# The opening of an attention and mixer kernel: small tables on GpSimd's queue, the first head loaded in halves

## The chip, the cores and the metric

The kernel runs on one core of one Trainium2 chip. A core has five engines that run side by side and meet only through semaphores: TensorE (PE) multiplies matrices into PSUM, VectorE (DVE) and ScalarE (ACT) do elementwise work, GpSimd (POOL) does some of that too, and SyncE (SP) issues transfers. SyncE, ScalarE and GpSimd each have a queue on which transfers (DMAs) are issued; all of them run on the same 16 DMA engines. The metric is the device time of one execution in microseconds (us).

## The reference

Two layers follow each other. The first is block-sparse attention over 4 batches of 8 heads, with 768 tokens of 64 elements and blocks of 32 tokens:

```python
scores = scale * np.matmul(q, k.transpose(0, 1, 3, 2))
mask = np.abs(blk_i - blk_j) <= window
mask = mask | (blk_i == 0) | (blk_j == 0) | (blk_i == n_blocks - 1) | (blk_j == n_blocks - 1)
for qb in range(n_blocks):
    for kb in sampled_blocks[qb]:
        mask[qb * block:(qb + 1) * block, kb * block:(kb + 1) * block] = True
scores = np.where(mask, scores, -1000000000.0)
attn = softmax(scores)
out = np.matmul(attn, v)
```

The 24 x 3 array sampled_blocks says which three extra key blocks each of the 24 query blocks sees. Its values are known only at run time, so the mask is computed on the chip.

The second is a residual mixer on the result x (4 x 768 x 512):

```python
a1 = alpha1 * x + beta1
u = x + lam * einsum('ts,bsd->btd', w_tok, a1)
a2 = alpha2 * u + beta2
out = u + lam * (np.maximum(a2 @ w_ch1, 0.0) @ w_ch2)
```

## The kernel before

**Stages.** Two heads make a pair, and there are 16 pairs. For a pair, q and k are brought to 16-bit types (tile rel), transposed (tiles qx and kx, 64 rows for the head dimension), multiplied to scores in PSUM (L601, later L611), turned into exponentials by ScalarE (L622, tile eT) and multiplied with v (L638). The token product of the mixer (L740) and its two channel products (L805, L974, L884) follow, batch by batch, between the pairs. The order of all this work is one list, ORDER, written out by hand; each engine carries out its part of it in that order, and nothing reorders it at run time.

**The mask of the first pairs.** For the first five pairs the mask is part of the score product: qx and kx get 24 more rows (the slice MB, rows 64 to 87). In kx these rows say which block a key belongs to (the constant ind), in qx they hold 0 where the query may see the block and -400 where not. They are made in the prologue: block_mask (L320 and L326) compares sampi, the sampled blocks, with the block numbers in eqt, a table of block numbers and the fixed mask, and reduces to mbm, 24 x 24. Two products (mask_bias, L357) spread it over 768 tokens, one half each, and VectorE (L366) and ScalarE (L369) write the two halves to qx.

**The prologue around the change.** Only what runs ahead of the list is edited:

- SyncE issues q of the first head (L290), the identity for the transposes (identb, L292), sampi (L294), ind for kx of slot 0 (L296), then q and k of the second head (L297, L298). ScalarE issues k of the first head (L291), the table eqt (L293) and ind for slot 3 (L295), and then loads its function table.
- TensorE runs products with a zero tile, called fillers here (zero, L310): 7 of 512 columns and 2 of 128 ahead of the first transposes, 12 of 128 ahead of the first score.
- first_cast (L340 on ScalarE for k, L342 on VectorE for q) casts the first head in two halves of three slots of 64 elements each. Both halves of q come first on VectorE, then block_mask.
- TensorE transposes the first three slots (flatA), then the last three (flatB), and then makes the mask products. VectorE and ScalarE copy the parts to kx and qx (L363 to L371).
- GpSimd's first instruction of its own copies 24 elements of q to a tile called hold (L378), which is used for nothing else. It waits for the first q, so all loads that GpSimd issues behind it (v, k and q of the following pairs, the token weights wtk, later the channel weights) start only then. GpSimd has 8 completion semaphores in turn; a load waits for the one 8 places ahead of it.

Of the kernel before, what the change touches and what calls it, by code (L numbers as in the profile page):

```python
# [14 lines left out]
I32 = mybir.dt.int32  # L15
# [5 lines left out]
S = 768  # L21
D = 64
BLK = 32
NBLK = S // BLK
# [3 lines left out]
P = 128  # L28
NT = S // P
HS = S // 2  # L30
# [172 lines left out]
def kernel(  # L203
# [19 lines left out]
    nc = tc.nc  # L223
# [19 lines left out]
    tabs_dr = nc.inline_tensor(tabs_np, name="tabs_c")  # L243
# [10 lines left out]
    sampi = pp.tile([P, 2 * NR], I32, name="sampi", tag="sampi")  # L254
    identb = pp.tile([P, P], BF, name="identb", tag="identb")
    qx = [pp.tile([P, S], BF, name=f"qx{i}", tag=f"qx{i}") for i in range(NQB)]
# [10 lines left out]
    eqt = pp.tile([P, NR + 2, NBLK], FP, name="eqt", tag="eqt")  # L267
# [4 lines left out]
    MB = slice(D, KC)  # L272


    def pair_ap(src, b, n):
        return src[b, 2 * n : 2 * n + 2].rearrange("h (p o) d -> p h (o d)", o=NT)
# [4 lines left out]
    def bank(i, shape, dt=FP):  # L281
        t = psum[:, ts(i, 512)]
        if dt != FP:
            t = t.bitcast(dt)
        t = t[:, 0 : int(np.prod(shape[1:]))]
        return t if len(shape) == 2 else t.rearrange("p (o c) -> p o c", o=shape[1])

    q2f = wk.tile([P, 2, NT * D], FP, name="q2f", tag="hts", bufs=2)
    k2f = wk.tile([P, 2, NT * D], FP, name="k2f", tag="hts", bufs=2)
    nc.sync.dma_start(q2f[:, 0, :], pair_ap(q, 0, 0)[:, 0, :])  # L290
    nc.scalar.dma_start(k2f[:, 0, :], pair_ap(k, 0, 0)[:, 0, :])  # L291
    nc.sync.dma_start(identb[:], ident_dr.ap())  # L292
    nc.scalar.dma_start(eqt[MB, 0:2, :], tabs_dr.ap().rearrange("p (r c) -> p r c", r=2))  # L293
    nc.sync.dma_start(sampi[MB, :], sampled_blocks.bitcast(I32))  # L294
    nc.scalar.dma_start(kx[3][MB, :], ind_dr.ap())  # L295
    nc.sync.dma_start(kx[0][MB, :], ind_dr.ap())  # L296
    nc.sync.dma_start(q2f[:, 1, :], pair_ap(q, 0, 0)[:, 1, :])  # L297
    nc.sync.dma_start(k2f[:, 1, :], pair_ap(k, 0, 0)[:, 1, :])  # L298
# [10 lines left out]
    def zero(w, i):  # L309
        nc.tensor.matmul(bank(i, [P, w]), warm[:, 0:P], warm[:, 0:w], start=True, stop=True)  # L310

    for _ in range(7):
        zero(512, 6)
    for _ in range(2):
        zero(P, 6)
    for t in vext:
        nc.vector.memset(t[:, :, :, D:VW], 1.0)
# [1 line left out]
    def block_mask():  # L319
        nc.vector.tensor_tensor(  # L320
            out=eqt[MB, 2 : 2 + NR, :],
            in0=sampi[MB, 0 : 2 * NR : 2].unsqueeze(2).broadcast_to([NBLK, NR, NBLK]),
            in1=eqt[MB, 0, :].unsqueeze(1).broadcast_to([NBLK, NR, NBLK]),
            op=ALU.is_equal,
        )
        nc.vector.tensor_reduce(  # L326
            out=mbm[MB, :],
            in_=eqt[MB, 1 : 2 + NR, :].rearrange("p r c -> p c r"),
            axis=mybir.AxisListType.X,
            op=ALU.max,  # L330
        )

    rels = {0: wk.tile([P, 2, NT, 2 * D], BF, name="rel", tag="rel", bufs=4)}

    def first_cast(a, lo=0, hi=NT):
        for i, src in enumerate((q2f, k2f)):
            sl = src[:, a, :].rearrange("p (o d) -> p o d", o=NT)[:, lo:hi, :]
            dst = rels[0][:, a, lo:hi, i * D : (i + 1) * D]
            if a == 0 and i == 1:
                nc.scalar.copy(out=dst, in_=sl)  # L340
            else:
                nc.vector.tensor_copy(out=dst, in_=sl)  # L342

    def transposes(rel, a, i, slots=range(NT)):
        tps = bank(i, [P, NT, P], BF)
        for o in slots:
            nc.tensor.transpose(tps[:, o, :], rel[:, a, o, :], identb[:])  # L347
        return tps.rearrange("p o c -> p (o c)")

    first_cast(0, 0, 3)  # L350
    first_cast(0, 3, 6)
    block_mask()
    bqs = {}

    def mask_bias(w):
        bqs[w] = bank((2, 7)[w], [P, 512])[0:NBLK, 0:HS]
        nc.tensor.matmul(bqs[w], mbm[MB, :], kx[3][MB, ts(w, HS)], start=True, stop=True)  # L357

    flatA = transposes(rels[0], 0, 0, range(0, 3))
    flatB = transposes(rels[0], 0, 1, range(3, 6))  # L360
    mask_bias(0)
    mask_bias(1)
    nc.vector.tensor_copy(out=kx[0][0:D, 0:P], in_=flatA[D:P, 0:P])  # L363
    nc.scalar.copy(out=qx[0][0:D, HS:S], in_=flatB[0:D, HS:S])
    nc.vector.tensor_copy(out=qx[0][0:D, 0:HS], in_=flatA[0:D, 0:HS])
    nc.vector.tensor_scalar(  # L366
        out=qx[0][MB, 0:HS], in0=bqs[0], scalar1=1.0, scalar2=BIG, op0=ALU.subtract, op1=ALU.mult
    )
    nc.scalar.activation(qx[0][MB, HS:S], bqs[1], AF.Identity, bias=-BIG, scale=BIG)  # L369
    nc.vector.tensor_copy(out=kx[0][0:D, P:HS], in_=flatA[D:P, P:HS])  # L370
    nc.vector.tensor_copy(out=kx[0][0:D, HS:S], in_=flatB[D:P, HS:S])  # L371
    for _ in range(12):
        zero(P, 6)
    for j in range(2, NQB):
        nc.sync.dma_start(qx[j][MB, :], qx[0][MB, :])

    hold = pp.tile([P, NBLK], BF, name="hold", tag="hold")
    nc.gpsimd.tensor_copy(out=hold[:], in_=q2f[:, 0, 0:NBLK])  # L378

    flag = pp.tile([P, 3 * NPAIRS], BF, name="flag", tag="flag")  # L380
    held = pp.tile([P, 3 * NPAIRS], BF, name="held", tag="held")
# [636 lines left out]
    for word in ORDER.split():  # L1018
        kind = word[: next(j for j, c in enumerate(word) if c.isdigit())]
        n, _, arg = word[len(kind) :].partition(":")  # L1020
# [35 lines left out]
```

## Time and profile before

| | us |
|---|---|
| runs: median of 3 (lowest to highest) | 293.21 (292.14 to 293.95) |
| profiled execution: time | 292.62 |
| profiled execution: span of the records | 290.8 |
| PE busy | 285.0 (98%) |
| DVE busy | 263.8 (91%) |
| ACT busy | 233.5 (80%) |
| POOL busy | 52.3 (18%) |

All durations come from the one profiled execution; its span is 1.8 us shorter than its time, for what lies around it. Four views are used. The chain of work that ended last goes back from the last instruction, at each step to what released it. The timeline lists instructions in order: start, length, engine, line, what is written from what, shape and count; a bracket says how long the engine sat idle before and what ended it. The DMA view gives each issue's size and its time to landing. The windows view gives busy time and DMA share for a stretch. A matmul's length in the timeline includes its way through the array, so the pace of products is read from start to start.

### The profile page before, as it was taken

The numbers are of one execution on the slowest core, as the hardware profiler recorded it, in microseconds if no ns is written. First come the engines' busy times: TensorE is split into PE (matmuls) and PEld (weight loads), VectorE is DVE, ScalarE is ACT, GpSimd is POOL, SyncE is SP. The second block draws the span as 40 slices with busy tenths as digits, with TensorE's granted clock in tenths as the row PEclk, the third lists the DMA queues.
The fourth block names the chain that finished last, engine by engine and source line by source line (L and its number), as shares of the span: only waits on it lengthen the run. The fifth ranks groups of instructions, "written<-read, shape, count | busy, mean of one in ns | idle before, by whom it ended". The sixth has DMA issues, their size and how long they took to land.

```text
span 290.8 us, 8517 instructions
## 1 busy us (share of the span) xinstructions
PE 285.0 (98%) x3542; PEld 214.8 (74%) x3542; DVE 263.8 (91%) x591; ACT 233.5 (80%) x349; POOL 52.3 (18%) x94
## 2 busy tenths in 40 slices
PE   8899999999999999999999999999999999999995
PEld 4677888665677788766677877888766788866884
DVE  5599998779999999999999999999999998699983
ACT  3999999849999999999999999968989860279400
POOL 5645754200521142024005000000000000000000
PEclk9999999999999999999999999999999999999999
DMA  6999999999684499499367002404210040330014
GB/s 161 178 233 223 196 206 190 203 218 182 120 112 30 53 119 135 77 176 116 43 183 146 9 2 56 83 5 47 38 74 0 16 115 0 148 144 1 2 42 176
DMA packets 48035, 30.97 MB, mean 107 GB/s; under 512 B 28972, under 2 KB 44092, under 8 KB 47996
## 3 DMA queue, kind: packets, MB, share of 16 engines
q0 software_dynamic: 15936, 15.21, 34.6%
q1 hardware_dynamic: 31412, 14.31, 23.0%
q10 hardware_dynamic: 648, 0.89, 0.9%
q8 instruction: 28, 0.46, 0.7%
q14 instruction: 11, 0.09, 0.1%
HBM read 31.19 MB, written 6.88 MB: 131 GB/s over the span
## 4 chain that ended last, share of the span: by engine, by line
PE 89%; ACT 8%; DVE 1%; issue 1%
PE psum L884 26%; PE psum L974 13%; PE psum L805 12%; PE psum L638 11%; PE psum L740 11%; PE psum L611 9%; ACT eT L622 6%; PE psum L601 4%; ACT hts L819 2%; PE psum L310 2%; PE psum L347 1%; PE psum L783 1%; DVE a1p L710 0%; PE psum L357 0%; ACT rel L396 0%
## 5 line engine op out<-in xcount | busy, mean ns | idle before, releaser
L622 ACT ACTIVATE eT<-psum 128x1024 f16<-128x1024 f32 (+1 forms) x145 | 140.1, 1028 | 9.4 <-PE psum L611 5.4
L632 DVE TENSOR_TENSOR eT<-eT,maskT 128x960 f16<-128x960 f16 x99 | 61.2, 650 | 0.0
L884 PEld LDWEIGHTS <-hts 128*128 128x128 bf16 x480 | 45.1, 98 | 8.5 <-issue 2.1
L638 PEld LDWEIGHTS <-eT 128*128 128x128 f16 x1152 | 44.4, 97 | 8.2 <-issue 1.7
L638 PE MATMUL psum<-vext,eT 128*128 128x65 f16 x1152 | 48.5, 193 | 0.0
L805 PE MATMUL psum<-uT,w1b 128*128 128x384 bf16 (+1 forms) x256 | 45.9, 327 | 0.1
L1000 ACT ACTIVATE snap<-psum,b1t 128x384 f32<-128x384 f32 x44 | 23.6, 581 | 17.7 <-PE psum L974 13.5
L740 PE MATMUL psum<-a1p,wtokT 128*128 128x128 bf16 x576 | 36.8, 219 | 0.2 <-DVE x_sb L749 0.2
L740 PEld LDWEIGHTS <-wtokT 128*128 128x128 bf16 x576 | 33.2, 98 | 4.1 <-DVE x_sb L749 0.8
L884 PE MATMUL psum<-w2t,hts 128*128 128x256 bf16 x288 | 35.8, 273 | 0.0
L843 DVE TENSOR_TENSOR x_sb<-x_sb,psum 128x256 f32<-128x256 f32 (+1 forms) x61 | 30.7, 514 | 4.7 <-PE psum L884 4.5
L805 PEld LDWEIGHTS <-w1b 128*128 128x128 bf16 x256 | 23.0, 98 | 16.1 <-ACT b1t L396 0.9
L819 ACT ACTIVATE hts<-psum,b1t 128x384 bf16<-128x384 f32 x53 | 29.1, 600 | 1.0 <-PE psum L805 0.5
L611 PE MATMUL psum<-qx,kx 64*128 64x256 bf16 x396 | 29.8, 272 | 0.0
L843 DVE TENSOR_TENSOR hts<-snap,psum 128x384 bf16<-128x384 f32 x48 | 24.7, 547 | 2.7 <-PE psum L974 2.3
L601 PE MATMUL psum<-qx,kx 88*128 88x512 bf16 (+1 forms) x120 | 25.7, 326 | 1.0 <-ACT eT L622 1.0
L884 PE MATMUL psum<-w2b,ss 128*128 128x256 bf16 x192 | 24.6, 273 | 0.0
L884 PE MATMUL psum<-w2b,hts 128*128 128x256 bf16 x192 | 24.4, 273 | 0.0
L611 PEld LDWEIGHTS <-kx 64*128 64x128 bf16 x396 | 15.2, 94 | 8.4 <-issue 3.7
L884 PEld LDWEIGHTS <-ss 128*128 128x128 bf16 x192 | 18.0, 98 | 3.8 <-issue 0.6
L749 DVE TENSOR_TENSOR x_sb<-x_sb,psum 128x384 f32<-128x384 f32 x32 | 17.4, 546 | 0.8 <-PE psum L740 0.5
L974 PEld LDWEIGHTS <-w1b 128*128 128x128 bf16 x128 | 12.1, 98 | 6.6 <-DVE hts L843 0.3
(98 smaller groups left out, 364.1 us busy)
## 6 DMA issues: line engine op xcount, KB each, us to landing
out_dram<-x_sb SPq DMA_DIRECT2D x17, 256.0 KB, 2.4
v<-in_v_dram POOLq DMA_DIRECT2D x16, 192.0 KB, 6.2
k<-in_k_dram POOLq DMA_DIRECT2D x15, 192.0 KB, 5.3
q<-in_q_dram POOLq DMA_DIRECT2D x15, 192.0 KB, 6.8
w2b<-in_moe_w_ch_dram POOLq DMA_DIRECT2D x4, 512.0 KB, 11.7
w1b<-in_moe_w_ch_dram POOLq DMA_DIRECT2D x4, 512.0 KB, 11.5
wtk<-in_moe_w_tok_dram POOLq DMA_DIRECT2D x3, 384.0 KB, 7.9
out_dram<-x_sb SPq DMA_DIRECT2D x2, 512.0 KB, 2.7
```

The lines of the kernel that those rows point to most:

```text
L601: nc.tensor.matmul(t[:, f : f + w], kx[h][0:KC, ts(jt, P)], qx[h][0:KC, c : c + w], start=True, stop=True,)
L611: nc.tensor.matmul(t[:, (2 * a + j) * TH : (2 * a + j + 1) * TH], kx[h][r, ts(2 * g + j, P)], qx[h][r, ts(th, TH)], start=True, stop=True,)
L622: nc.scalar.activation(eTs[n][:, c], t[:, c], AF.Exp, bias=EXPB, scale=SCALE)
L632: nc.vector.tensor_tensor(out=e, in0=e, in1=mask, op=ALU.min)
L638: nc.tensor.matmul(ops[key][:, t * VW : t * VW + D + 1], eTs[n][:, c : c + P], vext[n // NU % NV][:, a, jt, 0 : D + 1], start=(first and z ...
L740: nc.tensor.matmul(t[:, j, :], wtokT[:, s, ts(3 * g + j, P)], a1p[p][:, s, :], start=(s == 0), stop=(s == NT - 1),)
L805: nc.tensor.matmul(hps[i][:, 0:w], w1b[:, dk, ts(f, P)], uT[b][:, dk, hf * HS : hf * HS + w], start=(dk == 0), stop=(dk == 3),)
L819: nc.scalar.activation(hts[kk][:, f, :], t[:, 0:HS], AF.Relu, bias=b1t[:, f : f + 1], scale=1.0)
L843: nc.vector.tensor_tensor(out=out, in0=in0, in1=in1, op=op)
L884: nc.tensor.matmul(cps[b, q][:, side * HD : (side + 1) * HD], lhs[:, nk, :], rhs[:, nk, :], start=(z in (0, 6) and nk == 0), stop=(nk == H ...
L974: nc.tensor.matmul(chains[key], lhs[:, dk, ts(f, P)], rhs[:, dk, :], start=(z in (0, 1, 5) and dk == 0), stop=(dk == 1), skip_group_check= ...
L1000: nc.scalar.activation(dst, t, act, bias=bias, scale=1.0)
```

## The change

The two small loads that block_mask needs, sampi and eqt, move from SyncE's and ScalarE's queues to the head of GpSimd's queue, ahead of the copy to hold. The loads of the first head's q and k are each split into two transfers, of three slots each; the second halves are issued as the third transfer of their queues. The copy to hold reads the last 24 elements of q in place of the first 24.

On VectorE block_mask moves between the two casts of q. On TensorE the two mask products move between the transposes of the first half and those of the second, with three fillers of 128 columns ahead of them. ScalarE's mask bias (L369) moves ahead of its copy of the second half of q (L364). The fillers ahead of the first transposes become 4 of 512 columns and 3 of 128, and those ahead of the first score become 5.

```diff
-    nc.sync.dma_start(q2f[:, 0, :], pair_ap(q, 0, 0)[:, 0, :])
-    nc.scalar.dma_start(k2f[:, 0, :], pair_ap(k, 0, 0)[:, 0, :])
+    nc.gpsimd.dma_start(sampi[MB, :], sampled_blocks.bitcast(I32))
+    nc.gpsimd.dma_start(eqt[MB, 0:2, :], tabs_dr.ap().rearrange("p (r c) -> p r c", r=2))
+
+    def first_load(lo, hi):
+        cut = slice(lo * D, hi * D)
+        nc.sync.dma_start(q2f[:, 0, cut], pair_ap(q, 0, 0)[:, 0, cut])
+        nc.scalar.dma_start(k2f[:, 0, cut], pair_ap(k, 0, 0)[:, 0, cut])
+
+    first_load(0, NT // 2)
     nc.sync.dma_start(identb[:], ident_dr.ap())
-    nc.scalar.dma_start(eqt[MB, 0:2, :], tabs_dr.ap().rearrange("p (r c) -> p r c", r=2))
-    nc.sync.dma_start(sampi[MB, :], sampled_blocks.bitcast(I32))
     nc.scalar.dma_start(kx[3][MB, :], ind_dr.ap())
+    first_load(NT // 2, NT)
     nc.sync.dma_start(kx[0][MB, :], ind_dr.ap())
...
-    for _ in range(7):
+    for _ in range(4):
         zero(512, 6)
-    for _ in range(2):
+    for _ in range(3):
         zero(P, 6)
...
     first_cast(0, 0, 3)
+    block_mask()
     first_cast(0, 3, 6)
-    block_mask()
...
     flatA = transposes(rels[0], 0, 0, range(0, 3))
-    flatB = transposes(rels[0], 0, 1, range(3, 6))
+    for _ in range(3):
+        zero(P, 6)
     mask_bias(0)
     mask_bias(1)
+    flatB = transposes(rels[0], 0, 1, range(3, 6))
     nc.vector.tensor_copy(out=kx[0][0:D, 0:P], in_=flatA[D:P, 0:P])
-    nc.scalar.copy(out=qx[0][0:D, HS:S], in_=flatB[0:D, HS:S])
     nc.vector.tensor_copy(out=qx[0][0:D, 0:HS], in_=flatA[0:D, 0:HS])
...
     nc.scalar.activation(qx[0][MB, HS:S], bqs[1], AF.Identity, bias=-BIG, scale=BIG)
+    nc.scalar.copy(out=qx[0][0:D, HS:S], in_=flatB[0:D, HS:S])
...
-    for _ in range(12):
+    for _ in range(5):
         zero(P, 6)
...
-    nc.gpsimd.tensor_copy(out=hold[:], in_=q2f[:, 0, 0:NBLK])
+    nc.gpsimd.tensor_copy(out=hold[:], in_=q2f[:, 0, NT * D - NBLK :])
```

## The prediction

> **What bounds the kernel now.** I read the chain that ended last in order of time first, since the change touches only what runs before the first exponential. Start and length are in us.
>
> ```profile
> 1.19 3.38 PE psum L310 x9
> 4.57 0.64 PE psum L347 x6
> 5.21 0.74 PE psum L357 x2
> 5.95 1.15 PE psum L310 x12
> 7.10 0.23 PE psum L601
> ...
> 11.43 5.61 ACT eT L622 x6
> ...
> 25.52 1.03 ACT eT L622
> 26.55 0.05 issue
> 26.59 0.61 PE psum L601 x3
> ```
>
> Three stages: up to 7.1 us TensorE never stops, but two thirds of that time is filler (L310, products with a zero tile); then ScalarE's exponentials (L622) carry the chain; from 26.6 us on TensorE does, nearly to the end. A gain in the opening is worth only what reaches 26.6 us. The timeline tells what arrives there:
>
> ```profile
> 3.65 0.61 DVE L342 CAST rel<-q2f 128x192 bf16<-128x192 f32 x2 [2.42 <-DMA q2f<-in_q_dram]
> 3.68 0.20 POOL L378 CAST hold<-q2f 128x24 bf16<-128x24 f32 x1 [3.24 <-DMA q2f<-in_q_dram]
> 3.82 0.60 ACT L340 CAST rel<-k2f 128x192 bf16<-128x192 f32 x2 [0.35 <-DMA k2f<-in_k_dram]
> 3.83 0.84 POOL L414 DMA_DIRECT2D v<-in_v_dram  x1
> 4.32 0.23 DVE L320 TENSOR_TENSOR eqt<-sampi,eqt 24x72 f32<-24x72 int32 x1
> ...
> 19.75 0.51 PE L473 MATMUL psum<-identb,wtk 128*128 128x128 bf16 x6 [0.18 <-DMA wtk<-in_moe_w_tok_dram]
> ...
> 26.59 0.61 PE L601 MATMUL psum<-qx,kx 88*128 88x512 bf16 x3 [0.18 <-ACT eT L622]
> ```
>
> The brackets carry the argument. TensorE runs without a gap from 10.34 to 19.57 us, waits 0.18 us for a token-weight load, runs without a gap to 26.41, waits 0.18 us for ScalarE, and is the bound from there. So **two clocks arrive at 26.6 together**: the exponentials, which start with the first score, and GpSimd's stream of loads. The stream starts when the copy into hold (L378) sees the first q, and the DMA view has it full from then on (share 1.17 and 213 GB/s between 7.35 and 26.6 us): its loads land 5 to 10 us after issue, so a later start is a later landing.
>
> **The change, part by part.** Behind the prologue the instructions of every engine stand in the same order, so only its shift counts. Landing times below are the trace's landing records.
>
> *Halved loads.* Before, q was issued at 0.74 and landed at 3.63, k at 0.73 and 3.79 (2.9 and 3.1 us), the first packet 1.0 us after issue. Half the bytes take at least 1.0 for the start, half of the 1.5 us that the packets took, and 0.4 for completion: 2.15; at most the old 2.9. I take 2.5: first halves land at 3.25. ScalarE still issues three transfers and its table load (1.28, from 2.18) ends at 3.46, so k's first cast, not the load, sets the pace: 3.46 + 0.35, first transposes at about 3.9 instead of 4.36. The second q half is issued third on SyncE, where the sampled blocks were (1.64): landing between 3.8 and 4.4 by the same bounds. I take 4.0, near the lower one, because less lies ahead of it.
>
> *Blocks and table on GpSimd.* Two issues at about 0.73. GpSimd's one-dimensional issues take 0.54 to 0.58, the first load of all 0.84; the table is issued between 1.3 and 1.6. Issue to landing: the table on ScalarE's queue took 2.68 (1.18 to 3.86), the first GpSimd load 4.41 with 192 KB (3.83 to 8.25, first packet after 1.76). So the table lands between 4.0 and 6.0. It moves 4.5 KB, so the small load is the nearer row: 4.1.
>
> *Mask between the casts.* Call the start of the block comparison S: 4.1, where before it was 4.32. Now q's second cast is queued behind it on VectorE, and TensorE has the mask products ahead of the second transposes. From rows: comparison to reduction 0.26, reduction 0.31, on to the first product 0.25 (4.89 to 5.14), then 0.29 and 0.46 to what follows the second product, three transposes of 0.107 with 0.31 for the last to end, 0.06 and 0.47 for ScalarE's copy (L364, 5.24), 0.05 to the first score: S + 2.67 = 6.77. Before, it was 6.94: **0.17 us earlier**, break-even at S = 4.27. The second cast (S + 0.5 to S + 0.85) and VectorE's last key copy (before, 6.46 to 6.81, needed by later scores only) hide beside this. The k cast of the second half waits for its own half, 4.0 to 4.4, ahead of ScalarE's mask bias at S + 1.7, and is hidden.
>
> *Fewer fillers.* Out go 3 of 512 columns (0.427 each) and 3 net of 128 (0.107 to 0.056): 1.5 us of TensorE time. This is no gain of its own; it only lets the 0.17 us through, since before the 12 fillers ended at 6.94 while ScalarE's bias was done at 6.46. Their worth is the clock (below).
>
> *hold.* It now reads the last columns of q, the second half: 4.0 instead of 3.63. GpSimd's two added issues are done by 2.0, ahead of it. The stream starts **0.37 us later** (bounds 0.12 and 0.76), and v, k, q and the token weights queue behind.
>
> **Sum.** Exponentials: 26.59 - 0.17 = 26.42. Loads: 26.41 + 0.37 = 26.78. The later one decides: +0.19, 292.62 us of the profiled execution become 292.8. That execution lies 0.59 under the median of the runs (293.21), so on their scale **293.4 us**. Own range: stream bounds give 26.53 to 27.17, -0.06 to +0.58; with the spread of the runs shown (292.14 to 293.95) 292.6 to 294.2. No change that 1% (2.9 us, about what a measurement of this kernel can tell from no change) would show.
>
> **Rivals.**
>
> *A, gain kept (0.2).* The halves land at their lower bound (3.8) and the table at 4.0: stream +0.12, score 0.27 earlier. For it: packets at the opening move at 287 GB/s between 2 and 3 us, and less lies ahead of the halves. Against: the token-weight wait at 19.75, which caps any gain at 0.18 with the stream unmoved. Time: between -0.18 and +0.12, about 293.1.
>
> *B, TensorE stays slow (0.15).* Products start 427 ns apart for 512 columns and 107 for 128 until 6.60, 56 from 6.77 on: the pace doubles 5.5 us after the first product, though the granted-clock row shows 1.00 throughout. The fillers keep TensorE gapless until then. In the changed kernel they end at 3.2, transposes come at 3.9, and gaps follow before the products and the scores. If the 5.5 us count again from 3.9, the scores run at half pace from 6.8 to 9.4: 1.3 us of work lost. TensorE's idle stretch from about 9.4 to 10.34 takes up most, the exponential at 11.43 comes about 0.5 late: +0.5, 293.9; a second such stretch would cost up to 2 us more. Against: gaps of 0.4 to 0.7 us may not count. [...]
>
> *C, the table lands late (0.15), the slower side.* One mechanism: GpSimd's first transfers take the 4.41 us of its first load. It decides from S = 4.27. At S = 5.98 the first score comes at 8.65, 1.7 us late; the exponentials run back to back, and about 0.3 us of their waits at 17.0 to 25.5 are used up: +1.4, 294.6. q's second cast waits behind the comparison with all of VectorE. For it: a first packet after 1.76 against 1.02 on the other queues. Against: that load's 192 KB. [...]
>
> **Chances.** Forecast 0.5, A 0.2, B 0.15, C 0.15. The range reaches from A's low end to C: 292.3 to 294.8. Faster by over 1% needs more than the 0.18 us cap: 0.02. Slower by over 1% needs B's second stretch together with C: 0.07. Within 1%: 0.91.
>
> **What would show it.** Right: first score (L601) near 6.8, comparison (L320) near 4.1 and ended by the GpSimd load, hold near 4.0, the token-weight wait before 19.75 longer and later, TensorE reaching 26.4 without waiting for ScalarE. B: score products 213 ns apart for 256 columns instead of 109. C: VectorE idle ahead of L320 past 4.3. Wrong altogether: a difference that arises after 27 us, where nothing was moved.

## The result, and the profile after

The changed kernel is **slower by 1.0%**: 295.94 us median of 7 runs (294.75 to 297.26) against 292.99 us for the kernel before in the same runs, a ratio of 1.0098 with a 95% interval of 1.0073 to 1.0123. The forecast was 293.4 with a range of 292.3 to 294.8, so the time lies 1.1 us above the range. Its profiled execution took 295.44 us, with a span of 293.5 against 290.8.

The chain that ended last, of the changed kernel, in order of time (start, length, what; lines are those of the changed file, where L609 is the score product and L630 the exponential):

```profile
1.27 0.68 POOL sampi L290
1.96 3.03 DMA eqt<-tabs_c
...
5.08 0.24 DVE eqt L326
5.34 0.30 DVE mbm L332
...
7.61 2.74 PE psum L609 x9
10.36 0.64 PE psum L353 x6
10.99 0.85 PE psum L609 x2
11.85 0.80 PE psum L316 x2
12.65 1.61 PE psum L609 x5
14.28 5.61 ACT eT L630 x6
...
28.33 1.03 ACT eT L630
29.36 0.05 issue
29.41 0.61 PE psum L609 x3
```

Before, fillers held the chain to 7.1 us. Now it begins with the table's transfer on GpSimd's queue, and the stretch that ScalarE carried from 7.35 us on belongs to TensorE until 14.28. From there on the two chains are alike, piece by piece: six exponentials in 5.61 us at 14.28, before at 11.43 (2.85 us earlier); the first TensorE-bound scores at 29.41, before at 26.59 (2.82 earlier). The ends of the spans are 2.7 apart. **All of the loss arises before 14.3 us.**

The timeline of the changed kernel, for the same stretch (start, length, engine, line, what; idle time before it and what ended it):

```profile
1.27 0.70 POOL L290 DMA_DIRECT2D sampi<-in_sampled_blocks_dram  x1 [0.83 <-POOLq L1048]
1.96 0.55 POOL L291 DMA_DIRECT2D eqt<-tabs_c  x1
3.95 0.50 PE L353 MATMUL psum<-identb,rel 128*128 128x128 bf16 x3 [0.56 <-ACT rel L346]
4.68 0.20 POOL L386 CAST hold<-q2f 128x24 bf16<-128x24 f32 x1 [2.17 <-DMA q2f<-in_q_dram]
4.83 0.74 POOL L422 DMA_DIRECT2D v<-in_v_dram  x1
5.08 0.23 DVE L326 TENSOR_TENSOR eqt<-sampi,eqt 24x72 f32<-24x72 int32 x1 [1.67 <-DMA eqt<-tabs_c]
5.70 0.81 PE L363 MATMUL psum<-kx,mbm 24*24 24x384 bf16 x2 [0.93 <-DVE mbm L332]
7.61 2.74 PE L609 MATMUL psum<-qx,kx 88*128 88x512 bf16 x9
8.26 1.08 ACT L630 ACTIVATE eT<-psum 128x512 f16<-128x512 f32 x2 [0.73 <-PE psum L609]
```

and one line of the kernel before, for the same nine products:

```profile
6.94 1.47 PE L601 MATMUL psum<-qx,kx 88*128 88x512 bf16 x9
```

Two things are seen. The comparison starts at 5.08 in place of 4.32, behind the table, and the first score at 7.61 in place of 6.94: 0.68 us late. And the nine score products take 2.74 us, where before they took 1.47: TensorE works at half pace. In the single records the products start 427 ns apart for 512 columns until 13.85 us (before, 215), and the trace's clock record has its first step, to 1.0, at 13.87, where the kernel before has it at 6.71. The granted-clock row shows 1.00 for both kernels, since it fills the time ahead of the first step with 1.00; the pace has to be read from the starts.

So the 2.85 us are: 0.68 of late first score, 0.22 because the first product itself takes longer, and a remainder of 1.95 that builds up until 14.28, while TensorE runs at half pace. That the pace makes the remainder is tested below.

### The profile page after: what moved, and what is told of

Same layout as the page of the kernel before. It is cut to its first block, busy times and chain, and to the rows that moved or that the text cites. A ratio compares the mean times of both kernels' runs of the same rounds, so it can differ in the third digit from the quotient of the medians.

```text
span 293.5 us, 8508 instructions
## 1 busy us (share of the span) xinstructions
PE 287.0 (98%) x3536; PEld 215.4 (73%) x3536; DVE 263.2 (90%) x591; ACT 233.7 (80%) x349; POOL 52.8 (18%) x96
## 4 chain that ended last, share of the span: by engine, by line
PE 88%; ACT 7%; DVE 2%; DMA 1%; issue 1%; POOL 0%; DVEq 0%; POOLq 0%; ACTq 0%
PE psum L892 25%; PE psum L982 12%; PE psum L813 12%; PE psum L646 11%; PE psum L748 11%; PE psum L619 9%; PE psum L609 5%; ACT eT L630 5%; ACT hts L827 2%; DMA eqt<-tabs_c 1%; PE psum L353 1%; PE psum L791 1%; DVE a1p L718 0%; PE psum L316 0%; ACT rel L404 0%
## 5 line engine op out<-in xcount | busy, mean ns | idle before, releaser
L630 ACT ACTIVATE eT<-psum 128x1024 f16<-128x1024 f32 (+1 forms) x145 | 140.2, 1029 | 11.1 <-PE psum L619 5.4
L609 PE MATMUL psum<-qx,kx 88*128 88x512 bf16 (+1 forms) x120 | 28.1, 350 | 0.4 <-ACT eT L630 0.2
```

The costliest lines, as they stand in the source:

```text
L609: nc.tensor.matmul(t[:, f : f + w], kx[h][0:KC, ts(jt, P)], qx[h][0:KC, c : c + w], start=True, stop=True,)
L630: nc.scalar.activation(eTs[n][:, c], t[:, c], AF.Exp, bias=EXPB, scale=SCALE)
```

## The experiments

The theories: **clock** (TensorE's missed full pace carries most of the loss), **late table** (the loads delay the first score, and that is all) and **late stream** (GpSimd's later loads carry it). The table gives all kernels that were timed; z3_seven_again, one more profile of the kernel of y1_seven_late, was timed once, at 294.36 us. "First score" and "full pace from" are of each kernel's profiled execution, the latter from the trace's clock record where there is one. Most of these kernels' times scatter by 1 us or more, so a profile shows one execution and not the median; x3_gaps_filled and y4_halves_only were profiled in their longest one.

| kernel | ratio to before | 95% interval | first score | full pace from |
|---|---|---|---|---|
| before | 1 | | 6.94 | 6.71 |
| changed | 1.0098 | 1.0073 to 1.0123 | 7.61 | 13.87 |
| x1_loads_only | 1.0070 | 1.0043 to 1.0097 | 8.14 | 12.97 |
| x2_order_only | 1.0076 | 1.0041 to 1.0110 | 6.99 | 12.53 |
| x3_gaps_filled | 1.0061 | 1.0031 to 1.0092 | 8.08 | 5.10 to 8.51, again from 15.34 |
| x4_fewer_fillers | 1.0054 | 1.0035 to 1.0074 | 6.57 | 12.96 |
| y1_seven_late | 1.0025 | 0.9999 to 1.0051 | 6.68 | 5.95 (by the starts) |
| y2_dense | 1.0033 | 1.0018 to 1.0048 | 7.50 | 4.58 |
| y3_tables_gpsimd | 1.0053 | 1.0023 to 1.0084 | 8.03 | 9.99 |
| y4_halves_only | 1.0044 | 1.0022 to 1.0066 | 8.08 | 12.78 |
| z1_dense_hold_first | 1.0026 | 1.0010 to 1.0043 | 7.79 | 5.47 |
| z2_half_row_fillers | 1.0133 | 1.0094 to 1.0171 | 7.41 | 18.31 |
| w1_spread | 1.0012 | 0.9991 to 1.0033 | 6.82 | 5.75 |

### Fewer fillers alone

```diff
 (kernel before)
-    for _ in range(7):
+    for _ in range(4):
         zero(512, 6)
-    for _ in range(2):
+    for _ in range(3):
         zero(P, 6)
...
-    for _ in range(12):
+    for _ in range(5):
         zero(P, 6)
```

> The kernel before with nothing altered but its fillers, which become those of the changed kernel: 4 of 512 and 3 of 128 columns in front, 5 before the first score. Clock theory: a gap from 3.2 to 4.1 and another ahead of the scores keep the pace low; scores run 427 ns apart for 512 columns, 1 to 2.5 us over the kernel before. Late-table and late-stream theory: the loads are unaltered, so no loss; the first score may come 0.4 us earlier, within 0.3 us of the kernel before or slightly faster.

Measured: 294.20 us median against 292.90, ratio 1.0054 (1.0035 to 1.0074). Its timeline:

```profile
3.81 0.20 POOL L378 CAST hold<-q2f 128x24 bf16<-128x24 f32 x1 [3.37 <-DMA q2f<-in_q_dram]
4.42 0.23 DVE L320 TENSOR_TENSOR eqt<-sampi,eqt 24x72 f32<-24x72 int32 x1
6.57 2.74 PE L601 MATMUL psum<-qx,kx 88*128 88x512 bf16 x9
9.74 1.06 PE L601 MATMUL psum<-qx,kx 88*128 88x512 bf16 x2
11.58 1.69 PE L601 MATMUL psum<-qx,kx 88*128 88x256 bf16 x5
```

No load, cast or copy was altered. The first score came 0.37 us **earlier** than before, as the late-table theory had it, and still the kernel is slower: the nine products take 2.74 us, as in the changed kernel, and full pace comes at 12.96. Work that computes nothing was worth 1.6 us here by the ratio (1.0054 of 292.9), 1.3 by the medians. The clock theory holds; late table and late stream cannot explain it.

### The old loads with the new order

The loads of the kernel before, and hold on the first elements, in the changed kernel, with its order and its fewer fillers:

```diff
 (changed kernel)
-    nc.gpsimd.dma_start(sampi[MB, :], sampled_blocks.bitcast(I32))
-    nc.gpsimd.dma_start(eqt[MB, 0:2, :], tabs_dr.ap().rearrange("p (r c) -> p r c", r=2))
...
-    first_load(0, NT // 2)
+    nc.sync.dma_start(q2f[:, 0, :], pair_ap(q, 0, 0)[:, 0, :])
+    nc.scalar.dma_start(k2f[:, 0, :], pair_ap(k, 0, 0)[:, 0, :])
...
-    nc.gpsimd.tensor_copy(out=hold[:], in_=q2f[:, 0, NT * D - NBLK :])
+    nc.gpsimd.tensor_copy(out=hold[:], in_=q2f[:, 0, 0:NBLK])
```

> The old loads with the new order (mask between the casts, mask products between the transposes) and the new, fewer fillers. The comparison can start near 4.3 as before. Clock theory: the fillers end at 3.2, gaps follow, so the scores run at half pace (427 ns for 512 columns) past 10 us; 1.5 to 2.5 us over the kernel before. Late-table theory: no loss, since the table lands at 3.9 as before; within 0.3 us of the kernel before, or faster.

Measured: ratio 1.0076. The comparison starts at 4.37 and the first score at 6.99, as before; still the pace is half until 12.53. Since the fillers are the few of the changed kernel, this run doesn't price the order alone. The new order brings the first score no earlier, because q's second cast and ScalarE's copy now stand behind the mask. The expectation of the clock theory holds.

### The new loads with the old order and the old fillers

The reverse: the changed kernel's loads, and its hold, in the kernel before (not printed here: the old table loads, which go, and the line of hold).

```diff
 (kernel before)
-    nc.sync.dma_start(q2f[:, 0, :], pair_ap(q, 0, 0)[:, 0, :])
-    nc.scalar.dma_start(k2f[:, 0, :], pair_ap(k, 0, 0)[:, 0, :])
+    nc.gpsimd.dma_start(sampi[MB, :], sampled_blocks.bitcast(I32))
+    nc.gpsimd.dma_start(eqt[MB, 0:2, :], tabs_dr.ap().rearrange("p (r c) -> p r c", r=2))
...
+    first_load(0, NT // 2)
...
+    first_load(NT // 2, NT)
```

> The loads of the changed kernel (tables on GpSimd's queue, halves, hold on the second half) with the old order on VectorE and TensorE and the old fillers (7 and 2, then 12). Clock theory (the loss is TensorE's slow pace, kept up by gaps in its opening): the table still lands near 5.0 and the first score comes near 7.4 to 7.6, but the 12 fillers and the longer front leave few gaps, so the pace should double before 9; about 0.5 to 1.0 us over the kernel before, far from 2.9. Late-table and late-stream theory (the loads alone carry the loss): 2.3 to 2.9 us over the kernel before.

Measured: ratio 1.0070, more than the clock theory had (0.5 to 1.0 us) and less than the others (2.3 to 2.9): a miss. The second casts wait to 5.13 for their halves, the comparison starts at 5.51, the first score at 8.14, and the 12 fillers did not bring full pace before 12.97. The late loads made gaps on TensorE (0.82 us ahead of the transposes at 5.71), and in this execution the pace came 6.26 us later than before (12.97 against 6.71): the two causes are not independent.

### Gaps filled, and filled more

```diff
 (changed kernel; x3_gaps_filled, in brackets y2_dense)
-    for _ in range(3):
+    for _ in range(10):      [10]
         zero(P, 6)
...
-    for _ in range(3):
+    for _ in range(13):      [20]
         zero(P, 6)
     mask_bias(0)
...
-    for _ in range(5):
+    for _ in range(8):       [12]
         zero(P, 6)
```

> The changed kernel with its gaps on TensorE filled and nothing else altered: 7 more fillers of 128 columns in front (to 3.94), 10 more ahead of the mask products (to 5.64), 3 more ahead of the first score (to 7.6). Clock theory: the pace doubles before 8.0, the first exponential comes near 8.2 and the rest follows as in the kernel before; 0.6 to 1.0 us over the kernel before. Late-stream theory: the loads come as late as in the changed kernel, so the loss stays near 2.9 us.

Measured: ratio 1.0061, between the theories. The profile is of the longest of the five executions (296.21 us; the others took 293.57 to 294.64). The table came at 5.5 in it, later than the fillers lasted. The windows view of it, us by us (busy time of PE, its weight loads, DVE, ACT and POOL, then granted clock, DMA share, GB/s), shows what followed the gaps:

```profile
5.00:6.00 1.00, 0.55 (x8) 0.38 (x6) 0.42 (x2) 0.35 (x1) 1.00 (x3) 1.00 0.65 223
...
7.00:8.00 1.00, 0.42 (x8) 0.24 (x5) 0.94 (x4) 0.64 (x2) 1.00 (x3) 1.00 1.24 163
8.00:9.00 1.00, 0.92 (x4) 0.47 (x5) 0.86 (x4) 0.50 (x2) 1.00 (x2) 0.76 1.15 164
9.00:10.00 1.00, 1.00 (x6) 0.69 (x5) 0.00 (x0) 0.59 (x2) 1.00 (x2) 0.50 1.14 137
```

Here the fillers had brought full pace at 5.10. Then TensorE was busy for 0.55 and 0.42 of two microseconds, and at 8.51 the granted clock fell to 0.50, until 15.34. The three steps lie 3.41 and 6.83 us apart, once and twice some 3.41; a stretch of 3.41 us counted from such a step, forward or back, is called a window below. With the gaps filled further, y2_dense:

> The changed kernel with so many fillers that TensorE has no gap even if the table lands at 5.5: 10 of 128 columns in front, 20 ahead of the mask products, 12 ahead of the first score. Clock theory: the pace doubles between 5 and 8 us and stays up, the first exponential comes between 8.2 and 8.8 (table and fillers late), and that delay of 0.9 to 1.4 us is all that is lost: 0.9 to 1.4 us over the kernel before. Late-stream theory (the loads of GpSimd, 1.0 us later, carry the loss): 2.5 us or more, and TensorE waits for token weights for more than 0.5 us.

Measured: 293.94 us, ratio 1.0033 (1.0018 to 1.0048): 1.0 us over the kernel before, with every load and every dependent instruction of the changed kernel as it was. Its timeline:

```profile
4.97 0.23 DVE L326 TENSOR_TENSOR eqt<-sampi,eqt 24x72 f32<-24x72 int32 x1 [1.30 <-DMA eqt<-tabs_c]
5.19 0.20 POOL L386 CAST hold<-q2f 128x24 bf16<-128x24 f32 x1 [2.68 <-DMA q2f<-in_q_dram]
7.50 1.54 PE L609 MATMUL psum<-qx,kx 88*128 88x512 bf16 x9 [0.44 <-DVE kx L378]
14.78 0.40 PEld L481 LDWEIGHTS <-wtk 128*128 128x128 bf16 x6 [0.53 <-DMA wtk<-in_moe_w_tok_dram]
```

Table and hold are as late as in the changed kernel, the nine products take 1.54 us, and **fillers gave back two thirds of the loss**, 1.9 of 2.9 us (1.0098 to 1.0033). TensorE's weight load now does wait for the token weights, 0.53 us at 14.78.

### The stream of loads by itself

```diff
 (y2_dense)
-    nc.gpsimd.tensor_copy(out=hold[:], in_=q2f[:, 0, NT * D - NBLK :])
+    nc.gpsimd.tensor_copy(out=hold[:], in_=q2f[:, 0, 0:NBLK])
```

> The changed kernel with the many fillers of the run before (10 of 128 columns in front, 20 and 12), and with hold reading the first half of q again, so that GpSimd's loads start near 3.1 instead of 4.7 to 5.2. If the later stream of loads cost part of what was left (1.0 us over the kernel before), the token-weight wait on TensorE goes and 0.3 to 0.6 us come back: 0.4 to 0.7 us over the kernel before, which is the late first score alone. If the stream costs nothing, 1.0 us stays; if the earlier loads slow the table and the second halves, it becomes more.

Measured: 293.77 us, ratio 1.0026 (1.0010 to 1.0043).

```profile
3.19 0.20 POOL L386 CAST hold<-q2f 128x24 bf16<-128x24 f32 x1 [0.67 <-DMA q2f<-in_q_dram]
7.79 1.53 PE L609 MATMUL psum<-qx,kx 88*128 88x512 bf16 x9 [0.30 <-DVE kx L378]
```

The stream starts 2 us earlier than in y2_dense, and no product for the token weights waits for a load. In the two profiles the spans are 0.8 us apart, but the timed medians only 0.17, and the intervals overlap: that the later stream costs anything is not settled. What is left, 0.8 us by the ratio, agrees with the late first score, 7.79 against 6.94, 0.85 us; no run tests that delay alone. All ten times lie between 293.49 and 294.00, closer together than any other kernel's.

### The parts of the loads

Tables on GpSimd's queue, and nothing else:

```diff
 (kernel before)
+    nc.gpsimd.dma_start(sampi[MB, :], sampled_blocks.bitcast(I32))
+    nc.gpsimd.dma_start(eqt[MB, 0:2, :], tabs_dr.ap().rearrange("p (r c) -> p r c", r=2))
     nc.sync.dma_start(q2f[:, 0, :], pair_ap(q, 0, 0)[:, 0, :])
...
-    nc.scalar.dma_start(eqt[MB, 0:2, :], tabs_dr.ap().rearrange("p (r c) -> p r c", r=2))
-    nc.sync.dma_start(sampi[MB, :], sampled_blocks.bitcast(I32))
```

> The kernel before with one part of the change: sampled blocks and table on GpSimd's queue. The table lands near 4.9 and the comparison starts at 4.9 to 5.1 instead of 4.32, so the first score comes 0.4 to 0.7 us late (the 12 fillers start behind the mask products). Clock theory: one new gap of 0.5 us ahead of the mask products; if the pace is missed 2 to 3 us slower, if it is kept 0.4 to 0.7 us slower. Late-stream theory: hold still reads the first elements, so the stream starts as before and the loss is at most 0.7 us.

Halves (and hold on the second), tables on their old queues:

```diff
 (kernel before)
-    nc.sync.dma_start(q2f[:, 0, :], pair_ap(q, 0, 0)[:, 0, :])
-    nc.scalar.dma_start(k2f[:, 0, :], pair_ap(k, 0, 0)[:, 0, :])
+    first_load(0, NT // 2)
     nc.sync.dma_start(identb[:], ident_dr.ap())
     nc.scalar.dma_start(eqt[MB, 0:2, :], tabs_dr.ap().rearrange("p (r c) -> p r c", r=2))
+    first_load(NT // 2, NT)
```

> The kernel before with one part of the change: halves of the first loads, and hold on the second half; tables on their old queues, old order, old fillers. The table load on ScalarE comes one issue later (to 3.9). The second halves land near 4.6 to 5.1, so the second casts and transposes come 0.5 to 1.0 us later than before, and the first score 0.3 to 0.7 us later. Clock theory: a gap of 0.5 to 0.9 us after the first transposes; if the pace is missed 2 to 3 us slower, if kept 0.3 to 0.7 us slower. Late-stream theory: hold comes 1.0 to 1.5 us later, so most of the 2.9 us is lost here whatever the pace.

Measured: 1.0053 and 1.0044. The ten times of each fall into two groups: with the tables moved, four from 293.52 to 293.69 and six from 294.61 to 297.39; with the halves, six from 293.59 to 294.01 and four from 294.82 to 295.66. The kernel before had 292.94, so the lower groups are near the case of the expectations in which the pace is kept, the upper ones near that in which it is missed. Both profiles are of upper groups (294.97 and 295.66). From their timelines, tables first, halves second:

```profile
1.27 0.70 POOL L290 DMA_DIRECT2D sampi<-in_sampled_blocks_dram  x1 [0.83 <-POOLq L1040]
5.41 0.23 DVE L320 TENSOR_TENSOR eqt<-sampi,eqt 24x72 f32<-24x72 int32 x1 [1.01 <-DMA eqt<-tabs_c]
8.03 2.44 PE L601 MATMUL psum<-qx,kx 88*128 88x512 bf16 x9
```

```profile
5.06 0.20 POOL L383 CAST hold<-q2f 128x24 bf16<-128x24 f32 x1 [4.62 <-DMA q2f<-in_q_dram]
5.46 0.22 DVE L325 TENSOR_TENSOR eqt<-sampi,eqt 24x72 f32<-24x72 int32 x1
8.08 2.77 PE L606 MATMUL psum<-qx,kx 88*128 88x512 bf16 x9
```

In these executions each part alone brings the first score past 8 us and half pace into the scores, and by the ratios each is a loss. Together, in x1_loads_only, they cost 0.70%, less than the sum of 0.97%; the intervals are too wide to settle that difference. The halves land late without GpSimd's tables (hold at 5.06), so it is not the tables that delay them.

### Seven late fillers, twice

```diff
 (kernel before)
-    for _ in range(12):
+    for _ in range(7):
         zero(P, 6)
```

> The kernel before with 7 in place of 12 fillers ahead of the first score, all else as it was. The first score should start near 6.6 instead of 6.94. Clock theory: the window that doubled the pace at 6.7 is nearly as full, so the pace still doubles there in most executions; 0 to 0.2 us faster, where the wait for token weights caps it; where the pace is missed, 1.3 us or more slower. Theory that fillers matter only by their length: 0.3 us faster.

> The kernel with 7 late fillers once more, for a second profile: its ten times fell into two groups, 292.3 to 293.2 and 294.3 to 295.1. Clock theory: a profile from the upper group has score products 427 ns apart for 512 columns until some 10 to 13 us, one from the lower group 215 ns apart from the start; nothing else differs.

The ten times of the first are 292.32, 292.74, 292.76, 292.96, 293.19 and then 294.26, 294.27, 294.61, 294.85, 295.06: half of them near the kernel before, half some 1.7 us above. The first profile is of the execution of 292.32, the second, of the same kernel, of one of 294.36 us. Their score products, in that order:

```profile
6.68 1.53 PE L601 MATMUL psum<-qx,kx 88*128 88x512 bf16 x9 [0.17 <-DVE kx L370]
```

```profile
6.84 2.41 PE L601 MATMUL psum<-qx,kx 88*128 88x512 bf16 x9 [0.54 <-DVE kx L370]
```

The same code, started at about the same instant, runs at full pace in one execution and at half pace in the other (which had it from 3.93, lost it at 7.34 and had it back at 10.76). As expected of the clock theory; so one profile alone doesn't tell what the opening costs.

### Fillers on half the rows

```diff
 (kernel before)
-        nc.tensor.matmul(bank(i, [P, w]), warm[:, 0:P], warm[:, 0:w], start=True, stop=True)
+        nc.tensor.matmul(bank(i, [P, w]), warm[0:D, 0:P], warm[0:D, 0:w], start=True, stop=True)
```

> The kernel before with its fillers, and those in the list, on 64 rows of the array instead of 128; as many products, as many columns, so no instant of TensorE's time changes. If the window asks only whether TensorE is occupied, the pace doubles as before and the time is that of the kernel before within 0.2 us. If it weighs the rows in use (score products of 88 rows kept TensorE occupied for 2.5 us in the changed kernel and the pace did not double), the windows in the opening are missed: 1.5 to 3 us slower.

Measured: 297.49 us, ratio 1.0133 (1.0094 to 1.0171), the slowest of all. That is 3.9 us by the ratio, more than the 1.5 to 3 us expected. TensorE is busy throughout from 1.2 to 7.0 us, as in the kernel before; from 6 us on the windows view has:

```profile
6.00:7.00 1.00, 1.00 (x11) 0.98 (x11) 0.97 (x3) 0.48 (x1) 1.00 (x3) 1.00 1.12 184
7.00:8.00 1.00, 1.00 (x7) 0.50 (x6) 0.75 (x3) 0.00 (x0) 1.00 (x2) 1.00 1.20 164
8.00:9.00 1.00, 1.00 (x6) 0.57 (x4) 0.00 (x0) 0.94 (x2) 1.00 (x2) 1.00 1.21 159
```

and full pace comes only at 18.31. In this kernel being occupied was not all that counted: with 64 in place of 128 rows in use by the fillers, and nothing else altered, full pace came 11.60 us later (18.31 against 6.71), and all four times (296.31 to 297.64) lie above all twelve of the kernel before in the same runs (292.19 to 294.32).

### A try at a better kernel

```diff
 (kernel before)
+    zero(P, 6)
     mask_bias(0)
+    for _ in range(2):
+        zero(P, 6)
     mask_bias(1)
...
-    for _ in range(12):
+    for _ in range(9):
         zero(P, 6)
```

> The kernel before with 3 of its 12 late fillers moved: one ahead of the mask products, two between them, nine behind; the first score should stay at 6.9 to 7.0. If some executions of the kernel before miss the pace in the opening too (its times reach from 292.1 to 294.4, those of the dense kernel with hold on the first half only from 293.5 to 294.0), fuller windows should make the upper times rarer: 0 to 0.4 us faster in the median. If they do not, the time stays within 0.2 us of the kernel before.

Measured: 292.77 us against 292.71, ratio 1.0012 (0.9991 to 1.0033): no difference, and 4 of its 12 times lie above 294. No run pointed to a kernel faster than the one before.

## Why the prediction was wrong

- **Where the time would arise: right.** The traces are alike from 14.28 us on, and the loss is in the opening.
- **Fewer fillers, "no gain of its own; it only lets the 0.17 us through": the step that failed.** The fillers' worth was named and put off to rival B, and left out of the sum. Cutting them alone brings the first score forward by 0.37 us and yet costs 1.6 us (x4_fewer_fillers), and adding more to the changed kernel gives back 1.9 of the 2.9 us (y2_dense).
- **Rival B: right in kind, mis-sized.** The 5.5 us from the first product to the doubled pace were counted from 3.9, which gave half pace to 9.4 and +0.5 us. It lasted to 13.87. The term measured 1.95 us up to 14.28, and the chance of 0.15 was far too low: every cut or gap that was tried brought it on in some executions at least. The steps were not counted from the first product: in two profiles of one kernel it starts at 1.18 and 1.19 us, and full pace comes at 5.95 in the one (y1_seven_late) and at 3.93 in the other (z3_seven_again). Within an execution they are 3.41 us or a multiple of that apart: 5.10, 8.51 and 15.34 in x3_gaps_filled, 3.93, 7.34 and 10.76 in z3_seven_again; and in the clock records of the kernel before and of the changed kernel the drop at the end of the span comes 283.31 and 279.89 us after the first step, 83 and 82 times 3.413. Counted back from 13.87 by 3.41, the changed kernel passed 10.46 and 7.05 without a step. No run shows what sets these instants.
- **The table, S = 4.1: 5.08.** The first issue on GpSimd came at 1.27, not 0.73 (the profile puts 0.83 us of idle queue down to its own sequencer, alike in all kernels with the tables there), the second at 1.96, and the table took 3.02 to land, not 2.68. That is rival C's slower side below its price, and within the bounds of 4.0 to 6.0, of which the sum took nearly the lowest. No run shows why the sequencer issues no earlier than 1.27.
- **From the comparison to the first score, 2.67 us: right.** It was 2.53 in the changed kernel and 2.62 in x2_order_only. With S right, the first score would have come out right too.
- **Halves: first half right (3.03, forecast 3.25), second wrong.** It landed at 4.62 where I took 4.0 and had 4.4 as the upper bound. Its first packet came 1.2 us after issue, against 1.0 for the first transfer, and its packets then spread over 1.4 us (2.85 to 4.22) where I took 0.75. The DMA share was 0.95 and 0.98 in the two half microseconds from 3.5 to 4.5, so "less lies ahead of it" was no reason for the lower bound; which of the other loads held it up stays open.
- **hold 0.37 us later: 1.0.** The token-weight wait that should have grown was not seen in the changed kernel, as everything ahead of it was later still. With the pace restored it was (0.53 us in y2_dense), but its cost is not settled.
- **Rival A** did not occur: on the way to the first score only the first half, its casts and its transposes came earlier than before.
- **The range.** From A's low end (-0.18) to C (+1.4) the terms give 293.0 to 294.6 around the median of 293.21. The rest of 292.3 to 294.8 is an allowance that the prediction does not work out.

## What to carry to other kernels

Products that compute nothing may carry the opening: cost them by the pace of what follows, not by their own length (fewer of them brought the first score 0.37 us forward and cost 1.6 us, x4_fewer_fillers), and count which rows they use (64 for 128 cost 1.3%, z2_half_row_fillers). A transfer that lands later in the opening can cost twice: in the changed kernel 0.68 us as the late first score, and with the gaps on TensorE, together with the fewer fillers, 1.95 us at half pace. Where full pace comes early in some executions and late in others, times can fall into two groups (292.32 to 293.19 and 294.26 to 295.06 in y1_seven_late), and only many runs tell a gain from luck.

## What the runs showed that I had not expected

- The pace does not follow TensorE's occupation alone. Fillers on 64 instead of 128 rows, as many products and columns as before, moved full pace from 6.71 to 18.31 us in the profiles and cost 1.3%. Score products of 88 rows kept the changed kernel's TensorE occupied from 7.61 to 10.15 without a step at 10.46.
- By an estimate of mine, made after the runs from the starts and shapes in the profiles, rows times time sorts the windows of the opening. Count for each product its columns at the pace it ran at, cut off at the next start, and weight that time by its rows over 128, the most that any product here has; lay windows of 3.41 us out from each execution's first step. The 16 windows of the profiled executions that ended in full pace hold 0.74 to 1.00 of a full window, those at half pace that ended without it at most 0.74. By occupation alone the two kinds overlap (0.80 to 1.00 against up to 0.99). The two windows that lost the pace hold 0.34 and 0.37, the thinnest that kept it 0.52. It stays an estimate: the two kinds touch at 0.74, a few records can be missing from a trace, and no run was made to test it.
- Full pace once reached was lost again after one window: in x3_gaps_filled 3.41 us after it came (5.10 to 8.51), with gaps of 0.61 and 0.66 us in between, and in z3_seven_again likewise (3.93 to 7.34), with gaps of 0.35 and 0.54 us.
- The kernel before may miss the early pace in some executions too. Its 77 times from all comparisons reach from 292.1 to 294.4, 19 of them above 293.5; the ten of z1_dense_hold_first, with its many fillers, span 0.5 us. None of its longer executions was profiled, so that they miss the pace is not shown.
